# Two halves of w_in split on VectorE instead of GpSimd, and eight more transposed banks copied by VectorE instead of ScalarE

## The chip, the core and the metric

The kernel runs on one core of a Trainium2 chip. The metric is the device time of one execution in microseconds; lower is better. The core has TensorE (PE in the rows, PEld for its weight loads), VectorE (DVE), ScalarE (ACT), GpSimd (POOL) and the DMA queues, here issued from SyncE (SP). SBUF is the working memory and PSUM holds TensorE's results in banks of 128 partitions by 512 floats.

## The reference

Three stages follow one another, all in float32, with 4 batches of 576 positions.

1. Attention with 8 heads of 64 dimensions and a block-causal mask in blocks of 64: `softmax(scale * q k^T + mask) v`. Its result, with the heads side by side, is `x` of 4 x 576 x 512.
2. A gated unit: `h = relu(x @ w_in)` with `w_in` of 512 x 1024. The left half of `h` is `u`, the right half `v`; `v` is normalized over its features, mixed over positions by `w_spatial` with a bias for each position, multiplied by `u`, and multiplied by `w_out`.
3. A feed-forward block: `x + relu(norm(x) * g_ln @ w_ch1) @ w_ch2`.

`w_in`, `w_out`, `w_ch1` and `w_ch2` are handed over in 64-bit floats, as pairs of 32-bit words, and the kernel makes 32-bit floats of them itself ("decode" below).

## The kernel before

**High and low parts.** Most products are made from operands that are split in two: a high part, which is the float32 rounded to TensorE's fp32r type, and a low part, the difference between the value and its high part. Each product is then three matmuls (`mm3`, lines 106 to 108): high by high, high by low, low by high. `split` (line 94) makes the two parts, with an engine chosen for each.

**Attention.** A loop over `u` (line 559) goes through 16 head pairs (4 batches by 4 pairs) of 7 units each. Unit 0 of a pair is the tail of 64 rows (`c == 4`); then come the row blocks `c` = 3, 2, 1, each for both heads, with 512, 384 and 256 plus 128 columns. Step `u` issues the scores of unit `u` into a PSUM bank `sc`, the masked maximum over it by VectorE (line 322) and the exponential by ScalarE (line 328), and, `D` = 2 units behind, the transposes of an earlier unit. These are TensorE matmuls into a PSUM bank `tr` of which there are two (line 378), and the bank is copied to SBUF, to `pH` for `c` >= 2 and to `pL` for `c` = 1. Who copies is decided on line 369: VectorE (line 370) for `c >= PLAN["ev0"]` in the first batch, that is in the pairs 0 to 3, and for `c >= PLAN["ev1"]` in the other batches; else ScalarE (line 372). With `ev0` = 3 the 128x384 banks of `c` = 2 go to ScalarE in the first batch, eight of them. The weighted sum with the values (`pv`, line 429) needs all parts of `pH`, then all of `pL`.

**Around each pair.** `prepare` splits q and k into `stack` (the low parts on GpSimd, lines 233, 245, 247), `reciprocals` sends the softmax sums through DRAM and back as `rb`, and `store_x` multiplies by them and splits `x` into `xT` (lines 439, 60 and 442, all on GpSimd). From the second batch on, the matmuls of `relu(x @ w_in)` for the batch before (`vps` for the value half, then `ups`) are placed between the units by `fill`.

**Decoding w_in.** `decode_in` (line 445) handles eight pieces of 128x512, four of the value half first. Each is loaded as word pairs (`raw`); ScalarE makes `m` from the high words (line 88), VectorE shifts the low words into `e`, a PSUM bank out of the three of pool `p_mm`, which also serves `pv`, `vps` and `ups` (line 89), and VectorE joins the two (line 90). `m` is a tile with tag `vr`, one of three that the normalization of the value half uses too. The joined result is written back to `m`, and `split` has GpSimd write both parts of `win` from it (lines 101 and 102). The eight pieces are issued at the units listed in `DECODE` (5, 8, 15, 22, 29, 33, 36 and 40; the first entry, 1, starts the loads).

**Order.** Within an engine the instructions stand in an order that is made ahead of time by a planner, which goes through the program with costs of its own; instructions marked `keep_in_program_order` (lines 88 and 89 of a decode among them) keep their place. At run time each engine works its list off in order. A changed list of costs can therefore change the order in places that a diff doesn't show.

Of the kernel before, what the change touches and what calls it, by code (L numbers as in the profile page):

```python
# [17 lines left out]

PLAN = {'mm': 3, 'sc': 3, 'tr': 2, 'D': 2, 'hi0': 'v', 'hi1': 's', 'klo0': 'g', 'klo1': 'g', 'qlo0': 'g', 'qlo1': 'g', 'xm0': 'g', 'xm1': 'g', 'xh0': 'g', 'xh1': 'g', 'xl0': 'g', 'xl1': 'g', 'dm': 'g', 'dh': 'g', 'ev0': 3, 'ev1': 2, 'rate': 24500.0, 'vrb': 3, 'ds': 2, 'dy': 1, 'raw': 5, 'yn': 2, 'ts': 3, 'ring': 8, 'wt': 2, 'cb': 1, 'hq': 8, 'packed': 4, 'plain': 3, 'pre': 8, 'py': 10, 'pyn': 4, 'dn0': 2, 'dnn': 5, 'vl': 'v', 'pace': 3, 'wd': 7, 'tl0': 'v', 'tl1': 'v', 'xe': 's', 'pt': 6, 'dstart': 7}


def f32(ap):
    return ap.bitcast(F32)
# [8 lines left out]
def tile_kernel(  # L34
# [14 lines left out]
    def E(k, p=None):  # L49
        k = PLAN[k if p is None else k + ("0" if p < 4 else "1")]  # L50
        return {"v": nc.vector, "g": nc.gpsimd, "s": nc.scalar}[k]

    def cp(k, p, out, src):
        e = PLAN[k if p is None else k + ("0" if p < 4 else "1")]
        if e == "v":
            nc.vector.tensor_copy(out, src)
        elif e == "s":
            nc.scalar.copy(out, src)  # L58
        else:
            nc.gpsimd.tensor_scalar(out, src, 1.0, 0.0, op0=ALU.mult, op1=ALU.add)  # L60
# [20 lines left out]
    def decode(raw, m, e, out, here=lambda ins: ins):  # L81

        low, high = raw[:, :, 0], raw[:, :, 1]
        here(nc.scalar.activation(m, f32(high), AF.Prelu, scale=2.0**-112, alpha=2.0**32))  # L88
        here(nc.vector.tensor_scalar(e, low, 29, None, op0=ALU.logical_shift_right))
        nc.vector.scalar_tensor_tensor(  # L90
            out.bitcast(U32), m.bitcast(U32), 3, e, op0=ALU.logical_shift_left, op1=ALU.bitwise_or
        )

    def split(src, hi, lo, high="s", low="g"):

        if high == "s":
            nc.scalar.copy(hi, src)  # L97
        elif high == "v":
            nc.vector.tensor_copy(hi, src)
        else:  # L100
            nc.gpsimd.tensor_scalar(hi, src, 1.0, 0.0, op0=ALU.mult, op1=ALU.add)
        {"v": nc.vector, "g": nc.gpsimd}[low].tensor_tensor(lo, src, f32(hi), op=ALU.subtract)  # L102
# [28 lines left out]
    at = tc.alloc_tile_pool(name="at", bufs=2, side="right")  # L131
    p_mm = tc.alloc_tile_pool(name="p_mm", bufs=PLAN["mm"], space=PSUM, side="left")
    p_sc = tc.alloc_tile_pool(name="p_sc", bufs=PLAN["sc"], space=PSUM, side="right")
    p_tr = tc.alloc_tile_pool(name="p_tr", bufs=PLAN["tr"], space=PSUM, side="right")

    win = [xw.tile([128, KD, 2 * F], F32R, name=f"win{i}") for i in range(2)]
# [3 lines left out]

    PACKED = PLAN['packed']
    nat = {}
# [302 lines left out]
    def decode_in():  # L445
        raws = {}

        def fetch(i):
            if i < 2 * KD:
                h, kc = 1 - i // KD, i % KD  # L450
                raws[i] = dn.tile([128, F, 2], U32, tag="hl", name="raw", bufs=3)
                nc.sync.dma_start(
                    out=raws[i].rearrange("p a b -> p (a b)"), in_=wi32[:, kc, 2 * F * h:2 * F * h + 2 * F]
                )

        fetch(0)
        fetch(1)
        fetch(2)
        yield
        for i in range(2 * KD):  # L460
            h, kc = 1 - i // KD, i % KD
            m = dn.tile([128, F], F32, tag="vr", name="dm", bufs=PLAN["vrb"])
            e = p_mm.tile([128, F], F32, tag="mm", name="de").bitcast(U32)
            cols = slice(F * h, F * h + F)
            decode(raws.pop(i), m, e, m, tc.keep_in_program_order)
            split(m, win[0][:, kc, cols], win[1][:, kc, cols], PLAN['dh'])
            fetch(i + 3)
            yield

# [56 lines left out]
    dense = None  # L526
    debt = 0.0
    dec = decode_in()
    preps = {}

# [25 lines left out]
    D = PLAN['D']  # L556
    WARM = {2: 5, 3: 2, 4: 2, 5: 1}
    DECODE = {1, 5, 8, 15, 22, 29, 33, 36, 40}
    for u in range(NS + 8):
        p, i = divmod(u, NU)  # L560
# [142 lines left out]
    raws = {}  # L703
# [485 lines left out]
```

## Time and profile before

| | us |
|---|---|
| median of 3 runs | 794.83 |
| lowest and highest | 793.42, 795.38 |
| the profiled execution | 792.42 |
| its span, first to last instruction | 790.6 |
| TensorE busy in the span | 776.2 |
| VectorE busy | 506.7 |
| ScalarE busy | 428.9 |
| GpSimd busy | 416.7 |

The span is what the rows below cover. Attention fills the span up to about 256 us, with the matmuls of `w_in` among it from about 61 us on; the spatial mixing and `w_out` follow, then the feed-forward block from about 400 us to the end. The work of the change lies between 17 and 100 us.

### The profile page before, as it was taken

The page shows a single profiled execution, that of the slowest core. Times are in us where ns is not written, and L with a number is a line of the kernel's source. Part 1 is how long each engine was busy: PE and PEld are TensorE (multiplying, and loading weights), DVE is VectorE, ACT ScalarE, POOL GpSimd, SP SyncE. Part 2 cuts the span into 40 slices and gives each one's busy share as a digit, 9 for nine tenths or more (in the row PEclk, how much of TensorE's full clock was granted, in tenths as well). Part 3 has the DMA queues.
Part 4 walks back from the last instruction along what each step waited for, and adds up shares of the span by engine and source line. Part 5 has one row for each costly group of instructions (what it writes and reads, how often), then busy time and mean ns, then how long its engine had stood idle before and what let it go on. Part 6 is the DMA issues. An engine that isn't in the chain of part 4 may idle for free.

```text
span 790.6 us, 13252 instructions
## 1 busy us (share of the span) xinstructions
PE 776.2 (98%) x4504; PEld 668.5 (85%) x4508; DVE 506.7 (64%) x1165; ACT 428.9 (54%) x1051; POOL 416.7 (53%) x436
## 2 busy tenths in 40 slices
PE   9999999999999999899999999999999999999997
PEld 5666798778888899889988988889999898898996
DVE  6676646554463468776777778897566588555534
ACT  5889677777654464655444555553354454333421
POOL 5699866674621542232475565465545465555431
PEclk9999999999999999999999999999999999999999
DMA  8866456545321669778421332203010004000002
GB/s 250 208 178 180 132 162 173 134 133 154 112 97 64 200 209 282 233 240 282 135 81 30 109 102 85 77 31 130 1 37 18 0 1 136 12 0 1 1 1 80
DMA packets 53847, 88.70 MB, mean 112 GB/s; under 512 B 6930, under 2 KB 17298, under 8 KB 53780
## 3 DMA queue, kind: packets, MB, share of 16 engines
q1 hardware_dynamic: 53540, 87.55, 37.1%
q8 instruction: 35, 0.57, 0.3%
q10 hardware_dynamic: 240, 0.31, 0.2%
q14 instruction: 32, 0.26, 0.1%
HBM read 68.88 MB, written 18.95 MB: 111 GB/s over the span
## 4 chain that ended last, share of the span: by engine, by line
PE 83%; DVE 5%; DMA 5%; POOL 3%; ACT 2%; issue 2%; SPq 1%; ACTq 0%; POOLq 0%; DVEq 0%
PE hps L968 21%; PE o L106 8%; PE o L108 8%; PE o L107 8%; PE pv L429 5%; PE tr L378 4%; PE sc L309 3%; PE ups L106 2%; PE vps L106 2%; PE ups L108 2%; PE ups L107 2%; PE vps L107 2%; PE vps L108 2%; DMA raw<-in_w_ch_dram 2%; PE sc L306 2%
## 5 line engine op out<-in xcount | busy, mean ns | idle before, releaser
L102 POOL TENSOR_TENSOR a<-s,a 128x256 fp32r<-128x256 f32 x96 | 78.1, 818 | 91.1 <-ACT a L97 91.1
L107 PE MATMUL o<-w,h 128*128 128x512 f32 x288 | 112.2, 391 | 0.0
L106 PE MATMUL o<-w,h 128*128 128x512 f32 x288 | 106.8, 395 | 1.0 <-ACT h L960 1.0
L974 DVE TENSOR_TENSOR c<-hps,c 128x384 f32<-128x384 f32 x120 | 66.5, 554 | 51.6 <-PE hps L968 50.0
L108 PE MATMUL o<-w,h 128*128 128x512 f32 x288 | 96.4, 393 | 0.3 <-DVE h L961 0.3
L102 POOL TENSOR_TENSOR a<-w,a 128x256 fp32r<-128x256 f32 x72 | 61.5, 857 | 44.2 <-ACT a L97 38.4
L97 ACT CAST a<-s 128x256 fp32r<-128x256 f32 x96 | 38.4, 404 | 82.6 <-PE hps L968 75.6
L322 DVE CUSTOM_DVE_ANT_0 p<-sc,mask 128x512 f32<-128x512 f32 (+3 forms) x128 | 58.2, 485 | 34.6 <-PE sc L309 9.1
L328 ACT ACTIVATE p<-p,nm 128x512 f32<-128x512 f32 (+3 forms) x128 | 71.0, 557 | 14.1 <-DVE nm L322 11.9
L106 PEld LDWEIGHTS o<-w,h 128*128 128x128 f32 x288 | 53.8, 188 | 11.0 <-ACT h L960 2.3
L107 PEld LDWEIGHTS o<-w,h 128*128 128x128 f32 x288 | 54.1, 188 | 9.6
L370 DVE COPY pH<-tr 128x512 f32<-128x512 f32 (+1 forms) x88 | 49.0, 575 | 20.0 <-PE tr L378 19.8
L108 PEld LDWEIGHTS o<-w,h 128*128 128x128 f32 x288 | 53.2, 188 | 8.4 <-DVE h L961 1.2
L818 POOL TENSOR_TENSOR gt<-gf,gt 128x576 fp32r<-128x576 f32 (+1 forms) x17 | 24.6, 1445 | 63.1 <-ACT gt L817 60.1
L378 PE MATMUL tr<-idn,p 128*128 128x128 f32 x320 | 48.1, 277 | 0.5 <-DVE pH L370 0.3
L439 POOL TENSOR_TENSOR xx<-xx,rb 128x576 f32<-128x576 f32 x16 | 22.8, 1423 | 48.5 <-DMA rb<-r_d 42.3
L88 ACT ACTIVATE dm<-raw 128x256 f32<-128x256 f32 (+1 forms) x72 | 32.0, 464 | 27.8 <-DVE w2b L90 5.9
L961 DVE SCALAR_TENSOR_TENSOR h<-c,h 128x384 fp32r<-128x384 f32 x72 | 46.0, 658 | 1.6 <-ACT h L960 1.5
L245 POOL TENSOR_TENSOR stack<-qkt,stack 64x576 fp32r<-64x576 f32 x24 | 34.0, 1415 | 23.0 <-ACT stack L58 18.1
L117 POOL TENSOR_TENSOR rs<-rs,nhalf 128x1 f32<-128x1 f32 x36 | 22.4, 623 | 42.3 <-DVE rs L116 36.5
L960 ACT ACTIVATE h<-c 128x384 fp32r<-128x384 f32 x72 | 35.3, 521 | 17.2 <-DVE c L974 16.8
L378 PEld LDWEIGHTS tr<-idn,p 128*128 128x128 f32 x320 | 36.5, 140 | 8.8 <-DVE pH L370 4.4
(188 smaller groups left out, 2265.6 us busy)
## 6 DMA issues: line engine op xcount, KB each, us to landing
raw<-in_w_ch_dram SPq DMA_DIRECT2D x64, 256.0 KB
qkt<-in_qk_dram SPq DMA_DIRECT2D x110, 144.0 KB
vt<-in_v_dram SPq DMA_DIRECT2D x16, 320.0 KB
rb<-r_d SPq DMA_DIRECT2D x32, 144.0 KB
u_d<-ur SPq DMA_DIRECT2D x16, 288.0 KB
us<-u_d SPq DMA_DIRECT2D x16, 288.0 KB
y_d<-ys SPq DMA_DIRECT2D x18, 256.0 KB
yr<-y_d SPq DMA_DIRECT2D x18, 256.0 KB
```

The lines of the kernel that those rows point to most:

```text
L102: {"v": nc.vector, "g": nc.gpsimd}[low].tensor_tensor(lo, src, f32(hi), op=ALU.subtract)
L106: MM(out_ps, lhsT=a[0], rhs=b[0], start=first, stop=False)
L107: MM(out_ps, lhsT=a[0], rhs=b[1], start=False, stop=False)
L108: MM(out_ps, lhsT=a[1], rhs=b[0], start=False, stop=last)
L322: nc.vector.tensor_tensor_reduce(pt[:, o:o + n], src, m, -0.125, nm[:, 0:1] if c == 4 and i == 1 else 3e38, ALU.add, ALU.min, nm[:, i:i + 1],)
L328: nc.scalar.activation(pt[:, o:o + n], pt[:, o:o + n], AF.Exp, bias=nm[:, i:i + 1], scale=-1.0, accum_out=sm[:, col:col + 1])
L370: nc.vector.tensor_copy(out, src)
L378: nc.tensor.transpose(tr[:, o:o + 128], pt[:, 128 * kc:128 * kc + 128], idn)
L429: MM(ps[64 * j:64 * j + 64, a:z], lhsT=vt[:rows, kc, 64 * j:64 * j + 64], rhs=src[:rows, j, w * kc + a:w * kc + z] if part else src[:rows, ...
L961: nc.vector.scalar_tensor_tensor(t[:, 1], src, 0.0, f32(t[:, 0]), op0=ALU.max, op1=ALU.subtract)
L968: MM(ps, lhsT=a[x], rhs=b[y], start=not more and kc == 0 and k == 0, stop=kc == KD // 2 - 1 and k == 2, skip_group_check=True,)
L974: nc.vector.tensor_tensor(out, ps, x, op=ALU.add)
```

## The change

The joined 32-bit value is written to the PSUM bank `e` and no longer to `m`. VectorE makes the high part from that bank with a copy, and the low part with a subtraction of the bank and the high part. GpSimd has no part in `w_in` any more. With `ev0` = 2 the eight 128x384 banks of the pairs 0 to 3 are copied by VectorE as well.

```diff
-PLAN = {... 'ev0': 3, ...}
+PLAN = {... 'ev0': 2, ...}
...
             e = p_mm.tile([128, F], F32, tag="mm", name="de").bitcast(U32)
             cols = slice(F * h, F * h + F)
-            decode(raws.pop(i), m, e, m, tc.keep_in_program_order)
-            split(m, win[0][:, kc, cols], win[1][:, kc, cols], PLAN['dh'])
+            decode(raws.pop(i), m, e, e, tc.keep_in_program_order)
+            split(f32(e), win[0][:, kc, cols], win[1][:, kc, cols], "v", "v")
             fetch(i + 3)
             yield
```

## Rows read from the trace of the kernel before

**Rows 1.** The page: busy time, share of the span, instructions of each engine.

```profile
PE 776.2 (98%) x4504; PEld 668.5 (85%) x4508; DVE 506.7 (64%) x1165; ACT 428.9 (54%) x1051; POOL 416.7 (53%) x436
```

**Rows 2.** By stretch: length, busy PE, PEld, DVE, ACT, POOL (instructions), clock, DMA share.

```profile
15.00:60.00 45.00, 44.27 (x306) 31.39 (x310) 32.58 (x112) 37.60 (x105) 35.29 (x33) 1.00 0.75 210
60.00:100.00 40.00, 38.13 (x251) 28.48 (x247) 25.72 (x87) 31.46 (x81) 35.69 (x34) 1.00 0.55 155
...
110.00:260.00 150.00, 149.18 (x1067) 125.28 (x1064) 75.30 (x266) 98.16 (x259) 77.09 (x73) 1.00 0.42 122
```

**Rows 3.** Waits of TensorE's matmuls, 24 to 78 us: total, times, longest.

```profile
PE vps L106 <- POOL xT L60: 0.6, 1, 0.6
PE sc L309 <- DVE nm L322: 0.5, 1, 0.5
PE pv L429 <- ACT pH L372: 0.4, 1, 0.4
```

**Rows 4.** Waits of TensorE's weight loads, 24 to 78 us.

```profile
PEld sc L309 <- DVE nm L322: 1.8, 5, 0.7
PEld tr L378 <- DVE pH L370: 1.5, 5, 0.4
...
PEld tr L378 <- ACT pH L372: 0.5, 2, 0.3
```

**Rows 5.** GpSimd in order of time, 59 to 73 us: start, length, instruction.

```profile
59.43 1.42 POOL L439 TENSOR_TENSOR xx<-xx,rb 128x576 f32<-128x576 f32 x1
...
61.58 0.62 POOL L101 TENSOR_SCALAR win<-dm 128x512 fp32r<-128x512 f32 x1
...
66.58 1.27 POOL L102 TENSOR_TENSOR win<-dm,win 128x512 fp32r<-128x512 f32 x1
...
72.32 0.67 POOL L60 TENSOR_SCALAR xT<-xx 128x576 fp32r<-128x576 f32 x1
```

**Rows 6.** GpSimd by form, 15 to 110 us: busy, mean ns of one.

```profile
L102 POOL TENSOR_TENSOR win<-dm,win 128x512 fp32r<-128x512 f32 x8 | 10.3, 1283 | 0.3
...
L101 POOL TENSOR_SCALAR win<-dm 128x512 fp32r<-128x512 f32 x8 | 5.0, 620 | 4.3 <-DVE dm L90 4.0
```

**Rows 7.** VectorE by form and by tile: copies, the join, and a copy out of SBUF.

```profile
L370 DVE COPY pH<-tr 128x512 f32<-128x512 f32 x48 | 32.3, 685 | 17.9 <-PE tr L378 17.7
...
L370 DVE COPY pH<-tr 128x384 f32<-128x384 f32 x24 | 13.2, 552 | 1.7 <-PE tr L378 1.7
...
L90 DVE SCALAR_TENSOR_TENSOR dm<-dm,de 128x512 uint32<-128x512 uint32 x8 | 5.5, 683 | 0.2
...
L99 DVE CAST wo<-raw x4: 408/419/428, 272.9 to 285.3; 128x512 fp32r<-128x512 f32 x4
```

**Rows 8.** VectorE in order of time, idle before it in brackets.

```profile
40.95 0.68 DVE L90 SCALAR_TENSOR_TENSOR dm<-dm,de 128x512 uint32<-128x512 uint32 x1
41.86 0.69 DVE L370 COPY pH<-tr 128x512 f32<-128x512 f32 x1 [0.22 <-PE tr L378]
42.47 0.68 DVE L322 CUSTOM_DVE_ANT_0 p<-sc,mask 128x512 f32<-128x512 f32 x1
...
48.29 0.28 DVE L343 COPY rr<-rps 9x128 f32<-9x128 f32 x1 [1.06 <-PE rps L341]
...
73.06 0.69 DVE L90 SCALAR_TENSOR_TENSOR dm<-dm,de 128x512 uint32<-128x512 uint32 x1
73.78 0.70 DVE L89 TENSOR_SCALAR de<-raw 128x512 uint32<-128x512 uint32 x1
```

**Rows 9.** ScalarE in order of time.

```profile
57.89 0.41 ACT L249 CAST qtail<-stack 128x256 fp32r<-128x256 f32 x1 [0.85 <-POOL stack L245]
58.20 0.47 ACT L372 COPY pH<-tr 128x384 f32<-128x384 f32 x1
```

**Rows 10.** Busy time in two bursts of a pair, columns as in rows 2.

```profile
41.80:47.30 5.50, 5.50 (x38) 3.77 (x38) 5.37 (x17) 4.79 (x15) 4.92 (x7) 1.00 0.86 249
54.50:60.00 5.50, 5.05 (x35) 3.54 (x35) 5.38 (x17) 3.60 (x12) 5.20 (x5) 1.00 0.39 116
```

More of the change, by code (lines that the diff above doesn't have):

```diff
@@ L17 @@
 DRAM = bass.MemoryType.DRAM
-PLAN = {'mm': 3, 'sc': 3, 'tr': 2, 'D': 2, 'hi0': 'v', 'hi1': 's', 'klo0': 'g', 'klo1': 'g', 'qlo0': 'g', 'qlo1': 'g', 'xm0': 'g', 'xm1': 'g', 'xh0': 'g', 'xh1': 'g', 'xl0': 'g', 'xl1': 'g', 'dm': 'g', 'dh': 'g', 'ev0': 3, 'ev1': 2, 'rate': 24500.0, 'vrb': 3, 'ds': 2, 'dy': 1, 'raw': 5, 'yn': 2, 'ts': 3, 'ring': 8, 'wt': 2, 'cb': 1, 'hq': 8, 'packed': 4, 'plain': 3, 'pre': 8, 'py': 10, 'pyn': 4, 'dn0': 2, 'dnn': 5, 'vl': 'v', 'pace': 3, 'wd': 7, 'tl0': 'v', 'tl1': 'v', 'xe': 's', 'pt': 6, 'dstart': 7}
+PLAN = {'mm': 3, 'sc': 3, 'tr': 2, 'D': 2, 'hi0': 'v', 'hi1': 's', 'klo0': 'g', 'klo1': 'g', 'qlo0': 'g', 'qlo1': 'g', 'xm0': 'g', 'xm1': 'g', 'xh0': 'g', 'xh1': 'g', 'xl0': 'g', 'xl1': 'g', 'dm': 'g', 'dh': 'g', 'ev0': 2, 'ev1': 2, 'rate': 24500.0, 'vrb': 3, 'ds': 2, 'dy': 1, 'raw': 5, 'yn': 2, 'ts': 3, 'ring': 8, 'wt': 2, 'cb': 1, 'hq': 8, 'packed': 4, 'plain': 3, 'pre': 8, 'py': 10, 'pyn': 4, 'dn0': 2, 'dnn': 5, 'vl': 'v', 'pace': 3, 'wd': 7, 'tl0': 'v', 'tl1': 'v', 'xe': 's', 'pt': 6, 'dstart': 7}
 def f32(ap):
```

## The prediction

> **What bounds the kernel now.** I read the busy times first: TensorE is busy for 98% of the span, VectorE for 64%, GpSimd for 53% [rows 1]. So the change can only gain what TensorE loses to waiting near the work it touches, and can only lose what it adds to that waiting. Then the stretches. The eight decodes of w_in and the eight copies lie between 17 and 100 us. There TensorE stands still for 0.73 us in the first 45 us (45 - 44.27) and for 1.87 in the next 40 (40 - 38.13) [rows 2]; from 110 to 260 us it misses 0.82 of 150. In that later stretch it has matmuls in hand all the time, so whatever the early stretch wins or loses arrives at the end nearly whole.
>
> A busy matmul column hides short gaps, so the waits come next, those of the matmuls and those of the weight loads. For the matmuls between 24 and 78 us there are three: 0.6 us for GpSimd's xT, 0.5 for VectorE's maximum, 0.4 for ScalarE's copy of a c = 2 bank [rows 3]. For the weight loads it is VectorE that they wait for: 1.8 us for the maximum, which frees the score bank, and 1.5 for the copy that frees the transpose bank; ScalarE's c = 2 copies cost 0.5 [rows 4]. The reader is to see two things: everything that can be had is about 5.3 us (1.5 of rows 3 and 3.8 of rows 4, some of it told twice), and the larger part of it, 3.8 us (0.5 + 1.8 + 1.5), waits for the engine that is to get more work.
>
> **GpSimd's part.** It loses 8 x (0.620 + 1.283) = 15.2 us [rows 6]. Between 15 and 100 us it is busy for 35.29 + 35.69 = 71.0 us [rows 2], so it comes down to 55.8 of 85. Little of it is on TensorE's path. The place where it is: from 59.43 to 72.99 GpSimd runs without a pause, from the multiplication of pair 2 to the high part of pair 3, for which TensorE's first vps group waits 0.6 us; between them stand one L101 and one L102, 0.62 + 1.27 = 1.9 us [rows 3, 5]. Without them xT is there before TensorE asks, unless rb of pair 3, back through DRAM, is late. That gives 0 to 0.63; I take 0.6. A second place goes through ScalarE: its qtail at 57.89 waited 0.85 for GpSimd's stack, and the c = 2 copy stood behind it until 58.20 [rows 9]; TensorE's pv waited 0.4 for that copy [rows 3]. GpSimd earlier and the copy on VectorE both mend it: 0 to 0.4, I take 0.4.
>
> **ScalarE's part.** It loses eight copies of 0.47, 3.8 us [rows 9] out of 69.1 (37.60 + 31.46) [rows 2]. Of the 0.5 us that weight loads wait for such copies [rows 4] I take half, 0.25; 0 and 0.5 are the ends. The rest hides behind TensorE's own work.
>
> **VectorE's part.** It gets eight copies of 128x384 out of PSUM, 0.552 each, as the same copies in the other batches take [rows 7]. The high part is a 128x512 copy out of PSUM: 0.685, the row of the c = 3 copies. The low part is a subtraction with one input in PSUM and one in SBUF; the trace has no such form at this size, and the nearest row is the join, 0.683 for the same shapes and places [rows 7]. Its output moves from SBUF to PSUM, which I price at no change: the shift of line 89, which already writes that bank, takes 0.70 [rows 8]. Instructions overlap a little: a 128x512 copy of 0.69 that starts at 41.86 lets the next start at 42.47 [rows 8]. So a decode adds 2 x 0.61 = 1.2 us of queue, all eight 9.8; the copies add at most 8 x 0.552 = 4.4. That is 14.2 in all, and VectorE's 58.3 of 85 us (32.58 + 25.72) [rows 2] become 72.5, or 85%.
>
> The high part is read where reading is slow: the same 128x512 copy takes 0.419 us out of SBUF, for w_out [rows 7]. The Trainium skill has a rule on this, in VectorE: DVE Perf Modes, section Why PSUM operands drop a tier: a copy with an operand in PSUM loses the mode that moves two 32-bit elements a cycle. The rows agree, and by them the PSUM source costs 8 x (0.685 - 0.419) = 2.1 of the 14.2 us; with m as source it would be 12.1.
>
> Where the 14.2 us lie decides. Behind the join of the fourth decode VectorE idles 1.06 us before 48.29 [rows 8], and six of the eight decodes have such a pause of about a microsecond or more within two of their end; there the two new instructions cost nothing, except that the reciprocals' copy and what goes to DRAM behind it start up to 0.2 us later. The second and third decode have none. Behind the third, whose join starts at 40.95, stand 0.22 us of pause and then a burst without any until 48.29 [rows 8]: of 5.50 us VectorE is busy 5.37, TensorE all 5.50 [rows 10]. Queued there are the copies that free the transpose banks and the maxima that free the score banks, so TensorE waits for them, and ScalarE's exponentials and the pv of pair 2 behind them. The decode puts 1.2 - 0.22 = 1.0 us in, and the two c = 2 copies of that pair 1.1 more: 2.1 us. The 1.06 of pause takes its half back; of the other half TensorE has other matmuls to hide some. I take 0.6 for this burst, with 0 and 2.1 as its ends. The burst of pair 3 is as full, 5.38 of 5.50 [rows 10], but there the copy on VectorE takes the place of one that came late, and the cost is counted in the 0.4 above; its ends are 0 and 1.1. For the second decode and the copies of pairs 0 and 1, which have short pauses near them, I take 0.4 together, between 0 and 1.2 + 4 x 0.552 = 3.4.
>
> **PSUM bank and m.** The bank is now held until the low part is made, 1.2 us longer. When the sixth decode's join, started at 73.06, ends at 73.75, line 89 of the seventh follows at 73.78 [rows 8]; it will follow 1.2 us later, where VectorE has nothing better to do. I price it at 0; if a pv or vps stands behind it for a bank, it is 1.2 each. m comes free sooner, since line 102 of GpSimd no longer reads it; that tile waits on nothing that TensorE needs, so 0.
>
> **The sum.** Gain 0.6 + 0.4 + 0.25 = 1.25. Loss 0.6 + 0.4 = 1.0. The forecast is 0.25 us less, against the profiled execution's own 792.42 (span 790.6 and 1.82 around it): 792.2. The median of the runs lies 2.41 above that execution, so it should read 794.6. What the text above can't see is the planner: the new costs change the order on all engines, perhaps also far behind 100 us, by small amounts of either sign. A change of this kernel under 0.3%, 2.4 us, I count as none.
>
> **The rivals.**
>
> *GpSimd was the pace.* Between 59 and 73 us it runs without a pause [rows 5], and stacks, xT and the normalization all hang on it. Freed of 15.2 us, it may let the planner put the dense matmuls earlier, and nearly all that can be had comes: the waits on xT and pv, 1.0, the weight loads' 0.5, and, as ScalarE's exponentials come sooner, half of the 3.8 us for VectorE, 1.9: together 3.4 us, 791.4. For it speaks that GpSimd is the busiest of the three here, 71.0 of 85 us; against it, that TensorE waits for GpSimd once, 0.6 us, in 54 us of rows 3. Chance 0.28.
>
> *VectorE becomes the bound in the bursts.* This is the other side. The place is the start of each pair from 0 to 3, where maxima and copies come back to back [rows 10]. If each added instruction without a pause behind it passes on to TensorE, the price is 2.1 in the burst of pair 2, 1.1 in that of pair 3, and half of 3.4 in the pairs before, 4.9 in all; less the gains of 1.25 that is 3.7 more, 798.5. It decides when more than about half of the delays reach TensorE. For it speaks that its weight loads wait for VectorE already [rows 4]; against it, that TensorE itself is full in these bursts and its matmuls hide them. Chance 0.24.
>
> *A bank of PSUM is short.* The first vps group, waiting for xT [rows 3], keeps one of three banks meanwhile, and decodes, pv and the next vps share two. If the sixth and seventh decode each make one group wait 1.2 us and an earlier one does the same, 3.6 are lost; with the forecast's other terms that is 3.6 - 0.25 = 3.4 more, 798.2. Nothing in rows 3 shows a wait for such a bank today. Chance 0.05.
>
> **How the numbers follow.** The forecast gets 0.43, the rivals 0.28, 0.24 and 0.05. Faster by over 0.3% is the first rival, 0.28; slower is the other two, 0.29; the rest, 0.43, is no change. The likeliest case's own range is 792.4 to 797. The whole one, with 2 in 10 left out, takes in most of both rivals, 791.4 and 798.5, and the bounds of the burst: 790.8 to 798.6.
>
> **What the next profile would show.** GpSimd's busy time down by 15 us, VectorE's up by 14 to 15, ScalarE's down by 3.8. Line 102 for win on VectorE at about 0.69, line 99 for win at about 0.69, the join unchanged at 0.68. The matmuls' waits on xT at 72 us and on ScalarE's pH at 58 gone; new or longer waits of line 378's and 309's weight loads on VectorE between 40 and 60 us. The end of attention, where the last pv ends near 256 us, moved by as much as the end of the span. The forecast is wrong if TensorE's idle time between 15 and 100 us, 2.6 us now [rows 2], falls by more than the gains above or rises by more than 3 us, or if the difference comes from behind 260 us, where only the planner could have made it.

## The result, and the profile after

The changed kernel takes 799.56 us (median of 6 runs, 797.03 to 803.0), the kernel before 793.81 (6 runs beside them): a ratio of 1.0076 on record, interval 1.0059 to 1.0093 (ratios here and below are those on record, which differ a little from the quotient of two medians, here 1.0072). It is 5.7 us slower; the forecast was 794.6 and its range ended at 798.6. The profiled execution of the changed kernel took 798.84 us, with a span of 797.1 and a mean granted clock of 0.993, that is, the share of TensorE's full speed that it was granted (before: 790.6 and 0.999).

First the busy times, as in [rows 1].

```profile
PE 779.7 (98%) x4504; PEld 672.9 (84%) x4508; DVE 521.9 (65%) x1189; ACT 425.4 (53%) x1043; POOL 402.2 (50%) x420
```

VectorE is busy 15.2 us more, GpSimd 14.5 less, ScalarE 3.5 less: the work moved as the change says and nothing else was added. TensorE's list of matmuls is as long as before (4504 records in both), so the 6.5 us of span (797.1 - 790.6) are not added matmuls. The stretches of [rows 2], from the changed kernel; the column to read is the third from the end, the granted clock:

```profile
15.00:60.00 45.00, 43.45 (x274) 30.13 (x277) 34.84 (x110) 32.83 (x91) 27.05 (x24) 0.92 0.72 200
60.00:100.00 40.00, 37.00 (x246) 27.49 (x244) 32.95 (x98) 30.43 (x78) 27.20 (x24) 1.00 0.63 160
110.00:260.00 150.00, 148.63 (x1071) 125.66 (x1070) 78.97 (x279) 100.31 (x265) 78.15 (x73) 1.00 0.44 126
```

TensorE stands still for 1.55 us in the first stretch (0.73 before), and the clock there is 0.92, where before it was 1.00. To see where, compare the start of each pair's pv over pH in the two kernels. Before:

```profile
45.77 2.27 PE L429 MATMUL pv<-pH,vt 128*64 128x320 f32 x20
58.73 1.57 PE L429 MATMUL pv<-pH,vt 128*64 128x320 f32 x10 [0.39 <-ACT pH L372]
```

After:

```profile
50.79 4.32 PE L429 MATMUL pv<-pH,vt 128*64 128x320 f32 x20
64.25 2.00 PE L429 MATMUL pv<-pH,vt 128*64 128x320 f32 x14
```

The pv of pair 2 starts 5.0 us later, and its twenty matmuls take 4.32 us instead of 2.27. Pair 3 is 5.5 us late, and the last pv of the attention is 5.3 late (261.8 against 256.5). So 5.3 of the 6.5 us are made in the first pairs, nearly all of them between 35 and 55 us, and then carried to the end. The matmuls' waits from 24 to 78 us, the answer to [rows 3], name one place there:

```profile
PE vps L106 <- POOL xT L60: 1.6, 1, 1.6
PE sc L306 <- DVE nm L322: 1.5, 1, 1.5
```

The second line is the place. TensorE in order of time around it:

```profile
43.96 0.55 PE L378 MATMUL tr<-idn,p 128*128 128x128 f32 x3
46.05 0.79 PE L306 MATMUL sc<-stack 64*128 64x384 f32 x3 [1.55 <-DVE nm L322]
```

And TensorE by stretch in the same execution: length, busy (instructions), clock, DMA share, GB/s.

```profile
43.50:46.00 2.50, 1.00 (x6) 1.00 0.81 314
46.00:47.50 1.50, 1.45 (x8) 1.00 0.56 137
47.50:50.00 2.50, 2.50 (x13) 0.66 0.90 229
50.00:52.50 2.50, 2.50 (x13) 0.50 1.02 222
52.50:55.00 2.50, 2.50 (x16) 0.50 0.39 149
55.00:57.50 2.50, 2.50 (x21) 0.98 0.01 2
```

TensorE stands still for 1.55 us, works on at full clock for about 2 us, and then the granted clock falls to 0.50, the 1.2 GHz level, until about 55 us. The three slow rows lose 2.5 x (0.34 + 0.50 + 0.50) = 3.35 us. With the stand-still that is 4.9 of the 5.5 us. The Trainium skill (TensorE: Matmul & The Clock Gate, section Part 1: The HAM clock gate (the "warmup" mystery)) describes a clock of just these two levels, of which an idle engine gets the lower one. This trace agrees on the levels, 1.00 ahead of the stand-still and 0.50 behind it; but the lower one came only after about 2 us of work, and stayed while TensorE was busy all the time (2.50 of 2.50 us).

The other runs say the same. The mean granted clock of the six runs is 0.990 to 0.996, and what it costs, (1 - clock) x span, is 5.5 us on average; in the runs of the kernel before, in the four jobs of the experiments below, it is 0.8 to 1.0 us. By this estimate about 4.5 of the 5.7 us are lower clock, and only the rest is standing still and the like.

Now what TensorE waited for: the maximum of line 322, which frees the score bank. VectorE in order of time in the changed kernel:

```profile
42.91 0.69 DVE L370 COPY pH<-tr 128x512 f32<-128x512 f32 x1 [0.63 <-PE tr L378]
44.63 0.21 DVE L339 RECIPROCAL sm<-sm 128x9 f32<-128x9 f32 x1 [1.03 <-ACT sm L338]
44.77 0.63 DVE L102 TENSOR_TENSOR win<-de,win 128x512 fp32r<-128x512 f32 x1
45.31 0.68 DVE L322 CUSTOM_DVE_ANT_0 p<-sc,mask 128x512 f32<-128x512 f32 x1
```

ScalarE in the same stretch:

```profile
43.72 0.41 ACT L249 CAST qtail<-stack 128x256 fp32r<-128x256 f32 x1 [2.75 <-POOL stack L245]
44.03 0.36 ACT L58 COPY xx<-pv 128x256 f32<-128x256 f32 x1
44.30 0.30 ACT L338 ACTIVATE sm<-sm,tiny 128x9 f32<-128x9 f32 x1
44.50 0.76 ACT L328 ACTIVATE tail<-tail,nm 128x576 f32<-128x576 f32 x1
```

And ScalarE before:

```profile
41.07 0.35 ACT L58 COPY xx<-pv 128x256 f32<-128x256 f32 x1
41.32 0.78 ACT L328 ACTIVATE tail<-tail,nm 128x576 f32<-128x576 f32 x1
...
42.09 0.29 ACT L338 ACTIVATE sm<-sm,tiny 128x9 f32<-128x9 f32 x1
42.39 0.41 ACT L249 CAST qtail<-stack 128x256 fp32r<-128x256 f32 x1
```

The same four instructions stand in another order. Before, the cast to qtail (q at the last 64 positions, for the scores of the tail) came last; now it is first and waits 2.75 us for GpSimd's stack, with the small addition to the sums (L338) behind it. On VectorE the reciprocal, which needs those sums, now stands ahead of the maximum (before, the maximum at 42.47 came first [rows 8]). So the maximum comes at 45.31, 2.84 us later. Of these, 1.05 were lost before: the copy ahead of it starts at 42.91 instead of 41.86, because TensorE's transposes came that much later (42.22 instead of 41.17 us, behind the split scores of the third place below). Then 1.03 is the wait for the sums. New work of VectorE in front of the maximum is only L102, 0.54 of its 0.63 us, and it stands there because of its place in the list; the high part of that piece (L99) ran at 41.60, ahead of 0.63 us of idle time. And GpSimd, which has less to do, is late with the stack: it waited 3.01 us for rb before the multiplication of an earlier pair, began that at 34.44 us instead of 33.25, and the stack's L245 behind it ended at 43.69 instead of 42.36.

### The profile page after: what moved, and what is told of

The parts are those of the page before. It is cut to its first block, busy times and chain, and to the rows that moved or that the text cites. A ratio compares the mean times of both kernels' runs of the same rounds, so it can differ in the third digit from the quotient of the medians.

```text
span 797.1 us, 13256 instructions
## 1 busy us (share of the span) xinstructions
PE 779.7 (98%) x4504; PEld 672.9 (84%) x4508; DVE 521.9 (65%) x1189; ACT 425.4 (53%) x1043; POOL 402.2 (50%) x420
## 4 chain that ended last, share of the span: by engine, by line
PE 82%; DMA 6%; DVE 5%; POOL 3%; ACT 2%; issue 2%; SPq 0%; ACTq 0%; DVEq 0%; POOLq 0%
PE hps L968 21%; PE o L106 8%; PE o L108 8%; PE o L107 8%; PE pv L429 5%; PE tr L378 4%; PE sc L309 2%; PE ups L106 2%; PE ups L107 2%; PE ups L108 2%; PE vps L106 2%; PE sc L306 2%; PE vps L107 2%; PE vps L108 2%; DMA qkt<-in_qk_dram 2%
## 5 line engine op out<-in xcount | busy, mean ns | idle before, releaser
L102 POOL TENSOR_TENSOR a<-s,a 128x256 fp32r<-128x256 f32 x96 | 78.2, 818 | 91.5 <-ACT a L97 91.5
L102 POOL TENSOR_TENSOR a<-w,a 128x256 fp32r<-128x256 f32 x72 | 61.5, 856 | 44.0 <-ACT a L97 38.2
L370 DVE COPY pH<-tr 128x512 f32<-128x512 f32 (+1 forms) x96 | 53.8, 572 | 22.2 <-PE tr L378 21.9
L245 POOL TENSOR_TENSOR stack<-qkt,stack 64x576 fp32r<-64x576 f32 x24 | 33.9, 1414 | 30.5 <-ACT stack L58 29.6
```

## The experiments

Two theories. **A, the order**: the change itself costs nothing that can be measured; the planner, given other costs, put instructions in other places, some in front of work that they don't depend on, and TensorE's stand-stills there and the lower clock behind them are the loss. **B, VectorE's row of work**: the 14 us put on VectorE delay maxima and copies, as the rival of the bursts has it. Every ratio is against runs of the kernel before on the same chip in the same job.

### One part at a time

The decode alone is the changed kernel with 'ev0' put back to 3; the copies alone are the kernel before with this edit:

```diff
-PLAN = {..., 'ev0': 3, ...}
+PLAN = {..., 'ev0': 2, ...}
```

> The decode part alone (both parts of w_in on VectorE, ev0 back at 3). Theory A, order and clock: the changed kernel lost its time in one place, where ScalarE's queue had the copy to qtail, which waits for GpSimd's stack, ahead of the sums (line 338); VectorE's reciprocal, and behind it the maximum that frees the score bank, waited for these sums, TensorE stood still for 1.55 us, and its granted clock fell to half from 48 to 55 us, about 3.3 us more. In this kernel's lists the qtail copy stands behind the sums and behind the tail's exponential, so A expects no such stall, a clock of 1.00 from 45 to 56 us, and 793 to 795.5 us. Theory B, load: VectorE's added work itself delays TensorE, in proportion; the decode is 9.8 of the 14.2 us added, so 0.69 of 5.75 us, 797.8 us, with or without a fall of the clock.

> The copies alone (ev0 = 2, w_in split on GpSimd as before). Theory A: the qtail copy stands behind the sums in its lists, so no stall over 0.7 us between 40 and 60 us, and within 0.3% of the kernel before (791.5 to 796.2). Theory B: 4.4 of the 14.2 us added, so 0.31 of 5.75, 795.6 us, and longer waits for VectorE's maximum in the bursts at 42 and 55 us.

Measured: decode alone 795.83 us, 1.0032 (1.0018 to 1.0046); copies alone 793.15, 0.9997 (0.9985 to 1.0008). The parts do not add up to 1.0076: 0.47% belong to neither. In both, the clock is 1.00 from 35 to 60 us and the stand-still at 44 us doesn't exist. Both have another one, at TensorE's first value tile. The decode alone:

```profile
73.10 0.50 PE L106 MATMUL vps<-win,xT 128*128 128x512 f32 x1 [2.29 <-POOL xT L60]
```

### Mending the stand-still at 44 us in two ways

First, the order alone: in the changed kernel, qtail's cast is queued on ScalarE behind the addition to the sums.

```diff
+        with tc.issue_after(last_sm[0].ins):
             nc.scalar.copy(
                 view(qt, 0, [[192, 2], [256, 2], [1, 64]]), ...
             )
...
-        nc.scalar.activation(sm, sm, AF.Identity, bias=tiny)
+        last_sm[:] = [nc.scalar.activation(sm, sm, AF.Identity, bias=tiny)]
```

> The whole change, with the copy to qtail queued behind the sums (line 338) of the pair before on ScalarE; VectorE's work is the same as in the changed kernel. Theory A: the stall of 1.55 us and the half clock behind it are gone, 794 to 796.5 us; what is left over the kernel before is VectorE's load. Theory B: VectorE's load is the same, so 798 to 800 us.

Second, the clock alone: the order stays, but six matmuls of zeros are put in front of the stand-still.

```diff
-    ZEROS = {NU * p + i: n for p in range(4) for i, n in ((6, 1), (7, 2))}
+    ZEROS = {NU * p + i: n for p in range(4) for i, n in ((6, 1), (7, 2))} | {24: 6}
```

> The whole change, with six matmuls of zeros (6 x 0.22 = 1.3 us) on TensorE just ahead of the stall of 1.55 us, in front of the c = 2 scores of pair 3; the result is the same. It tells what the clock alone costs. If the clock falls because TensorE stands still there, the stall shrinks to about 0.3 us, the clock stays at 1.00 from 47 to 56 us, and 3 us come back: 796 to 797 us. If the clock is no part of it, or falls anyway, 799 to 800.5 us.

Measured: qtail behind 794.62, 1.0027 (1.0012 to 1.0043); zeros 796.56, 1.0049 (1.0037 to 1.0062). With qtail behind, from 45 us on (busy, clock as above):

```profile
45.00:50.00 5.00, 4.70 (x32) 1.00 0.64 205
50.00:55.00 5.00, 5.00 (x41) 1.00 0.78 219
72.00:76.00 4.00, 2.75 (x11) 0.61 0.87 242
```

With the zeros:

```profile
45.00:50.00 5.00, 4.60 (x30) 1.00 0.65 178
50.00:55.00 5.00, 5.00 (x41) 1.00 0.68 183
```

With qtail behind, the first two rows show the stand-still and the low clock at 45 us gone, with VectorE's work unchanged; the place of the qtail cast was worth 0.5%. The edit holds the cast in every pair, not in this one alone, and the lists of ScalarE and VectorE follow in a few places (here the reciprocal comes ahead of the copy, and L102 behind the maximum). The lists of TensorE and GpSimd are those of the changed kernel to the end, apart from four of the kernel's own filler matmuls of zeros, whose records the trace of the changed kernel lacks. With the zeros nothing but the six matmuls differs in any list. The stand-still shrinks to 0.40 us, the clock is 1.00 from 45 to 55 us, and the pv of pair 3 starts at 60.91 instead of 64.25 us: the clock's 3.35 us are back there, although the zeros are themselves work of no use. In the ratio they give back half of qtail's 0.5%; in the profiled execution the clock falls later instead (0.91 from 72 to 76 us and 0.67 from 76 to 80), behind a wait of 2.04 us of the value tile. That place is also what is left with qtail behind, where the row from 72 us on has 0.61:

```profile
73.25 0.79 PE L106 MATMUL vps<-win,xT 128*128 128x512 f32 x1 [2.60 <-POOL xT L60]
```

### The second place: the value tile

TensorE's list had the last three matmuls of the first value tile (kc = 3), which need the xT of pair 3, in front of transpositions and scores that need nothing of it. They are queued behind the pv of pair 4 instead, in four kernels: the change with qtail held too, before, the copies alone, the decode alone.

```diff
-            mm3(
-                ps, [x[:, kc, cols] for x in xT], [w[:, kc, F:2 * F] for w in win],
-                kc == 0, kc == KD - 1,
-            )
+            with tc.issue_after(last_pv[0].ins) if (pair, t, kc) == (0, 0, KD - 1) else nullcontext():
+                mm3(...)
```

> The full change; the cast of qtail is held behind the addition to the sums on ScalarE (as in the run before of that kind), and the last three matmuls (kc = 3) of the first value tile are held behind the pv matmuls of pair 4 on TensorE, where in the changed kernel they stood ahead of the transposes and waited 1.6 us (2.6 us with qtail held alone) for xT. Nothing of the work is left out. Theory A (the new order of the queues, and the clock that falls after a stand-still, are the whole cost; VectorE's 14 us lie in idle time): the wait of vps for xT falls under 0.3 us, the clock stays 1.00 from 35 to 100 us, ratio 0.995 to 1.000 (789 to 793 us). Theory B (VectorE's longer row of work itself costs something in the first batch, beside the order): ratio 1.002 to 1.004 still, though both waits are gone, and the start of the pv of pair 5 stays 1 to 3 us behind that of before.

> The kernel before with the last three matmuls of the first value tile held behind the pv matmuls of pair 4, the same edit as in the run beside it; nothing of the change. It is the control: in before this wait is 0.6 us and the clock is 1.00. Theory A: ratio 0.998 to 1.000. Theory B says the same of this kernel; what tells them apart is the difference between it and the full change with both holds: under A none (within 0.2%), under B 0.2 to 0.4%.

> The copies of the 128x384 banks on VectorE alone (w_in's parts as before), with the same hold of the first value tile. Copies alone gave ratio 0.9997 with 2.1 + 1.0 us of waits for xT and a clock of 0.62 in 76 to 80 us in its profile. Theory A: these waits and the dip go and the ratio falls to 0.996 to 0.999. Theory B: unchanged, 0.999 to 1.001.

> w_in's parts on VectorE from the bank alone (copies as before), with the same hold of the first value tile. The decode alone gave ratio 1.0032 with a wait of 2.3 us for xT at 73 us and a clock of 0.74 to 0.84 behind it. Theory A: the wait and the dip go, and with them 2 to 3 us: ratio 0.998 to 1.000. Theory B: the nine rows of four instructions on VectorE cost in themselves, ratio 1.002 to 1.004 still.

Measured: the full change with both holds 793.11 us, 0.9993 (0.9979 to 1.0008); before with the hold 792.71, 0.9986 (0.9978 to 0.9995); copies 791.98, 0.9974 (0.9961 to 0.9988); decode 793.54, 1.0008 (0.9993 to 1.0023). The full change with both holds, where the row of 72 us stood at 0.61:

```profile
72.00:76.00 4.00, 3.49 (x29) 1.00 0.92 240
```

Two places in two queues are the 0.76%: with them mended, VectorE has the same 15 us more, the kernel takes the time of before within the interval (0.15% either way), and the pv of pair 5 starts at 91.13 us, before at 91.00. Theory B fails here. The control, before with the hold, is itself 0.14% faster than before; the full change stands 0.07% behind it, inside both intervals.

### The third place, and what stayed open

With the decode on VectorE the list had the transposition of the reciprocals (rps) of pair 5 in front of that pair's pv; in the decode with one hold:

```profile
91.53 0.38 PE L342 MATMUL rps<-idn,sm 128*9 128x128 f32 x1 [2.05 <-ACT pL L373]
```

The third hold queues it behind pv, as before has it:

```diff
-        nc.tensor.transpose(ps[:9, :128], sm, idn)
+        with tc.issue_after(last_pv[0].ins) if p == 5 else nullcontext():
+            nc.tensor.transpose(ps[:9, :128], sm, idn)
```

> The full change with the two holds, and a third: the transposition of the reciprocals of pair 5 (rps) is held behind the pv matmuls of that pair, as it stands in before; in both kernels with the decode on VectorE it stood ahead of pv and waited 1.0 to 2.0 us at 89 us for a PSUM bank that ScalarE's copy of pL frees. Nothing of the work is left out. Theory A (order alone): the wait goes, pv of pair 5 starts about 1 us earlier, and the ratio goes from 0.9993 to the 0.997 to 0.998 of the copies with one hold. Theory B (what is left of the decode's cost, 0.2% beside the copies alone, is VectorE's row of work): ratio stays 0.999 to 1.001.

> w_in's parts on VectorE alone, with the hold of the first value tile and the same hold of rps. With the first hold alone the ratio was 1.0008, with a wait of 2.0 us for pL at 89 us and a clock of 0.91 in 80 to 100 us. Theory A: both go, ratio 0.997 to 0.9985. Theory B: 1.000 to 1.0015 still.

> The copies on VectorE with the hold of the first value tile, once more, so that it stands beside the two others on one chip. Its ratio was 0.9974; 0.996 to 0.999 is expected by both theories.

Measured on one chip: full change with three holds 792.70, 0.9992 (0.9981 to 1.0003); decode with two holds 791.05, 0.9971 (0.9957 to 0.9984); copies again 792.78, 0.9985 (0.9973 to 0.9997). For the decode theory A was right: 0.32% above before became 0.29% below it, with the same work on the same engines. For the full change it was wrong; the third hold brought nothing. It also moved more than rps: from 91 us on TensorE's list is dealt anew. Between the two kernels the pv of pair 2 differs by 1.4 us already (48.77 and 47.40 us), and the score matmuls explain most of it. The full change with three holds, TensorE by form up to 66 us:

```profile
L309 PE MATMUL sc<-stack 64*128 64x384 f32 x24 | 5.6, 376 | 0.1
L309 PE MATMUL sc<-stack 64*128 64x512 f32 x18 | 4.8, 425 | 0.0
```

The decode with two holds:

```profile
L307 PE MATMUL sc<-stack 64*128 64x384 f32 x24 | 6.4, 377 | 0.0
L307 PE MATMUL sc<-stack 64*128 64x512 f32 x18 | 2.9, 427 | 0.0
```

Eighteen matmuls of the same size take 4.8 or 2.9 us; one group of the 64x384 goes the other way, 5.6 against 6.4, so 1.1 us net. The three of head 0 use rows 0 to 63 of the array, those of head 1 rows 64 to 127, and where both groups stand side by side they run together. TensorE in order of time in before shows six in the time of three:

```profile
40.26 0.97 PE L306 MATMUL sc<-stack 64*128 64x512 f32 x6
```

In the changed kernel the same six are split, by one of the tail's transpositions and a pv:

```profile
39.38 0.96 PE L306 MATMUL sc<-stack 64*128 64x512 f32 x3
...
41.33 0.96 PE L306 MATMUL sc<-stack 64*128 64x512 f32 x3
```

The Trainium skill says of small matmuls (TensorE: Matmul & The Clock Gate, section Part 3: Packing small matmuls — row/col tiling) that several of them run concurrently in the array when each has tiles of its own; 0.97 us for the six against 0.96 + 0.96 agrees. The next runs put the groups of pairs 2 and 3 side by side again:

```diff
+                    with tc.issue_after(pv_low[1].ins) if u == 22 else nullcontext():
                         held = MM(out, lhsT=st[rows, x, 0, q], rhs=st[rows, y, 1, 0:nn], ...)
+                if u == 16:
+                    tc.add_manual_dep(first_tr[u - 7].ins, held.ins.name, ...)
```

> The full change with the three holds, and the score matmuls of units (j = 0, c = 3) and (j = 1, c = 3) side by side on TensorE in pairs 2 and 3, as they stand in before. The traces so far: the three 64x512 matmuls of one head take 0.96 us alone, and those of both heads together 0.97 us where no transposition stands between them; in the full change two of three such groups are split (4.8 us for 18 matmuls up to 66 us, 2.9 us in before and in the decode alone). Nothing is left out. Theory A (order alone): 18 matmuls in 2.9 to 3.0 us, the kernel 1 to 2 us shorter than with three holds (ratio 0.9992), so 0.9965 to 0.998. Theory B (VectorE's row of copies and parts together is what holds the full change at 0.9992): ratio 0.999 to 1.000 still, the time turned into waits on VectorE.

> The decode alone with two holds once more (ratio 0.9971), beside the others on one chip. Both theories: 0.996 to 0.9985.

> The copies alone with the hold of the first value tile (0.9974 and 0.9985 in two jobs), and the score matmuls of both heads of pair 3 side by side (they are split there: 3.9 us for 18 matmuls, 2.9 us in before). Theory A: 0.8 to 1 us less, ratio 0.996 to 0.998. Theory B: 0.998 still.

Measured: joined in the full change 794.58, 1.0008 (0.9988 to 1.0028; single runs from 789.86 to 800.16); decode again 792.37, 0.9987 (0.9973 to 1.0002); copies joined (with the edit of u == 22 alone) 796.79, 1.0035 (1.0018 to 1.0051). Theory A was right at the place (in the full change eighteen matmuls in 2.9 us) and wrong in the total. The pv of the joined kernel:

```profile
47.71 2.28 PE L442 MATMUL pv<-pH,vt 128*64 128x320 f32 x20
59.11 2.27 PE L442 MATMUL pv<-pH,vt 128*64 128x320 f32 x20
72.74 2.28 PE L442 MATMUL pv<-pH,vt 128*64 128x320 f32 x20
91.55 3.54 PE L442 MATMUL pv<-pH,vt 128*64 128x320 f32 x20 [1.69 <-ACT p L340]
```

Pair 2 starts 1.06 us earlier than with three holds (48.77), pair 4 still 1.07 earlier (73.81). At 91 us the lead is gone: pv waits 1.69 us for an exponential, the clock is 0.83 from 90 to 100 us, and again 0.83 from 330 to 340. In the copies joined the clock is 0.66 in that last stretch. It is the clock that takes back what was won: (1 - clock) x span averages 3.2 us over the twelve runs of the joined kernel and 0.7 with three holds (before in the same jobs: 1.0 and 0.8). An estimate from the mean times without it puts the joined kernel 1.3 us below before and the one with three holds 0.6, so the scores side by side won about 0.7 us of the 1 to 2 expected. What holds the full change at 0.9992, while the decode alone comes to 0.9971, is not settled. The two repeats (0.9971 and 0.9987, 0.9974 and 0.9985) say that jobs differ by 0.1 to 0.2%, so differences under that are not read here.

The best versions are the decode with two holds (791.05 and 792.37 us) and the copies with one (791.98 and 792.78): both 0.1 to 0.3% faster than before, and about 1% faster than the change as it was made (0.9971 or 0.9987 against 1.0076). Before with the first of these holds is at 0.9986, so by these figures at most 0.15% of it comes from the moved work, which is no more than jobs differ.

## Why the prediction was wrong

**The prices were right.** The forecast took 0.685 for the high part, 0.683 for the low part, no change for the join (0.683) and 0.552 for the copies. Measured, from 15 to 110 us:

```profile
L370 DVE COPY pH<-tr 128x384 f32<-128x384 f32 x12 | 6.6, 548 | 0.9 <-PE tr L378 0.9
...
L90 DVE SCALAR_TENSOR_TENSOR de<-dm,de 128x512 uint32<-128x512 uint32 x8 | 5.5, 688 | 0.1
L99 DVE CAST win<-de 128x512 fp32r<-128x512 f32 x8 | 5.4, 679 | 0.1
L102 DVE TENSOR_TENSOR win<-de,win 128x512 fp32r<-128x512 f32 x8 | 5.4, 670 | 0.0
```

**The burst behind the third decode**: the forecast named this place, 0.6 us with 2.1 as its end, as a delay by work. The loss there was 4.9 us of stand-still and clock, and work was not its cause: both are gone when qtail moves behind the sums (1.0076 to 1.0027). What stays is 1.05 us at the pv of pair 3 (59.78 against 58.73), and one split group of scores, 0.96 us, accounts for about that much.

**GpSimd's 0.6 us on xT** did not come; the wait grew to 1.6 us. The forecast had the condition in it, "unless rb of pair 3, back through DRAM, is late". GpSimd in order of time:

```profile
63.43 1.42 POOL L439 TENSOR_TENSOR xx<-xx,rb 128x576 f32<-128x576 f32 x1 [5.46 <-DMA rb<-r_d]
...
74.59 1.42 POOL L439 TENSOR_TENSOR xx<-xx,rb 128x576 f32<-128x576 f32 x1 [1.59 <-DMA rb<-r_d]
76.10 0.67 POOL L60 TENSOR_SCALAR xT<-xx 128x576 fp32r<-128x576 f32 x1
```

GpSimd, freed of 14.5 us, waits for rb. These rows alone don't show it, since all of pair 3 is 5.5 us late in this kernel. But with both holds the pv of pair 3 is at 59.65, 0.9 us behind before, and xT still starts at 72.84 instead of 72.32, after a wait of 2.10 us for rb. So xT hangs on the reciprocals' way through DRAM, and GpSimd's speed doesn't help. The value tile, placed earlier in TensorE's list, made that a longer wait.

**The waits for ScalarE's pH** (0.4 and 0.25) are gone, as forecast: none of the matmuls' two waits above names it. The weight loads' waits for VectorE grew in exchange: between 24 and 78 us those of the scores for the maximum are 3.2 us (2.3 + 0.9), before 2.0 (the 1.8 of [rows 4] and 0.2). The forecast's "everything that can be had", 5.3 us, was also short: [rows 4] leaves out 0.8 us of weight loads waiting for xT and three times 0.6 us for the maximum, pL and pH.

**The step that failed** is the last of the sum: the planner's new order was put at "small amounts of either sign", that is at zero, and the sum has no term for TensorE's clock, which all its prices take at 1.00. Together they were the result. Two instructions in front of others cost 0.49% and 0.34% (1.0076 to 1.0027 to 0.9993), a third 0.2 to 0.4% in the decode alone (1.0008 to 0.9971, or 0.9987 in the second job); and of the 4.9 us at the first of them 3.35 were the lower clock behind 1.55 us of standing. The forecast's own alarm shows what it missed: it watched TensorE's idle time between 15 and 100 us, which rose by only 1.95 us (from 2.60 to 1.55 + 3.00), under its 3, because TensorE counts as busy at half clock too. The direct sum, 0.25 us gained, is not contradicted by the full change with two of the places mended (0.07 to 0.08% less than before, 0.6 us), but that is too little to tell from none, and its terms were not measured one by one.

**The rivals.** VectorE as the bound in the bursts gave 798.5 us, near to the 799.56 measured; that is luck, since the holds refute its reason. GpSimd as the pace falls with the waits for rb. No wait for a PSUM bank of the decode shows among TensorE's matmuls.

**Behind 260 us** the forecast held that only the planner could make a difference. In the changed kernel 1.4 us more are lost from 320 to 340 us (the delay grows from 5.3 to 6.7), where the clock is 0.83 from 330 us on, behind a wait of 2.42 us for VectorE's yn (the normalized rows of the feed-forward block). But no instruction's place differs: from 280 us on the four engines work off the same lists in both kernels. VectorE stands still ahead of yn for a load of `w_ch`, in before and in the changed kernel:

```profile
326.80 0.30 DVE L89 TENSOR_SCALAR raw<-raw 128x256 uint32<-128x256 uint32 x1 [0.64 <-DMA raw<-in_w_ch_dram]
332.17 0.29 DVE L89 TENSOR_SCALAR raw<-raw 128x256 uint32<-128x256 uint32 x1 [2.06 <-DMA raw<-in_w_ch_dram]
```

The clock there isn't a matter of the kernel alone. The decode with two holds ran in two jobs: 1.61 us of waiting for yn at 1.00 in one profiled execution, 1.86 us and 0.66 from 327 to 332 us in the other. Why the load comes later was not tested.

## What to carry to other kernels

Where a planner orders the queues by estimated costs, moving work from one engine to another can deal all queues anew, and that can outweigh the work itself (here 5.7 us, against less than 1 once two places were mended): before judging the edit, find the first matmul that stands still in the new trace, see which queue has an instruction in front that waits for something unrelated, hold it back, and time again. On a kernel whose TensorE is busy 98% of the time, price a new stand-still of a microsecond and a half with the clock that may fall behind it, here 1.55 + 3.35 us, and read the granted clock beside the idle time, which doesn't show it. And look at what stands beside what: of matmuls on different halves of the rows the second half cost nothing only while they were neighbours.

## What was not expected of the hardware

- A stand-still of 1.55 us ahead of 46.05 us was followed by the 1.2 GHz level (0.50) for nearly seven us; one of 1.58 us at 76.8 in the same execution was followed by none (1.00 from 72 to 80 us). With three holds even 2.20 us at 328.96 were followed by 1.00 (325 to 345 us). The length of a stand-still alone does not tell, nor does the kernel: the decode with two holds had 1.00 in one execution and the lower level in another, behind nearly the same wait.
- Six 64-row matmuls of 512 columns in 0.97 us where the two heads are neighbours, three in 0.96 where they are not; over the first 66 us that is 2.9 against 4.8 us for eighteen.
- GpSimd with 14.5 us less to do delivered xT of pair 3 no earlier even where the pairs ran within 1 us of before: with both holds it started at 72.84, before at 72.32 [rows 5], because rb arrived when it did (2.10 us of waiting for it).
